# Selection matmuls beside the scores, lent PSUM banks, one routed group held back, zero matmuls at the start: sigmoid attention with mixture of depths

## The chip, the core and the metric

The kernel runs on one core of a Trainium2 chip. The time is device microseconds of one execution. Three runs of the kernel before gave 525.93, 521.94 and 525.99 us; the median is 525.93 us.

## The reference, cut to what matters

```python
# q, k, v: (8, 12, 448, 64) float32          B, H, S, Dh
scores = scale * (q @ k.transpose(0, 1, 3, 2)) - log(S)
attn   = 1 / (1 + exp(-scores))              # sigmoid, no softmax
x      = (attn @ v) transposed to (8, 448, 768)

# mixture of depths: per batch, 128 of the 448 tokens are routed
s   = x . w_gate                             # (8, 448)
top = the 128 tokens with the largest s
h   = relu(x[top] @ w1)                      # w1 768 x 1024
out = x;  out[top] = x[top] + sigmoid(s[top]) * (h @ w2)   # w2 1024 x 768
```

Everything is float32. The attention has 96 heads; the routed part has eight batches of 128 rows.

## The kernel before, in words

**Steps and units.** The work is written out by hand: every engine's instructions are issued in program order. Four heads of one batch make a group (24 groups, three to a batch), and two groups make a *step* (12 steps, numbered 0 to 11; what follows step 11 is called step 12). A step has seven *units*, numbered 0 to 6. `unit(s, n)` writes scores of 128 keys for four heads into two PSUM tiles of two banks each (16 matmuls; the trace counts each as two) and reads each tile with one sigmoid on ScalarE (L210). Units 0 to 2 belong to the step's first group, 4 to 6 to its second, unit 3 to both.

**Between the units.** `gap(s, n)` puts other TensorE work behind unit n: in gaps 0 to 2 the rest of the attention times v of the step before (`values`, L237), in gaps 3 to 5 routed work, in gap 6 the first part of `values` of this step. `values` fills two PSUM tiles o0 and o1; after its last part VectorE reads them (`take`, L252) and they are free again. PSUM holds four such tiles in all: two that rotate for the scores (`psc`), and o0 and o1, which `values` and the routed work share. `banks("o")` hands out o0 and o1 in turn. In step 0 units 1, 3 and 5 use o0 and o1 for their scores.

**Routing of a batch b.** When its third group is done, `store` writes x to a scratch in HBM and to the output (8 DMAs on SyncE's queue) and `gate` makes the scores. In gaps 4 to 6 of the same step (batch 0: 5 and 6) follow `spread` (one matmul, L289), `rank` for four blocks of tokens (two VectorE instructions each, L306 and L309) and `place` (builds the 0/1 matrix `sel`, L318). In the next step comes `select`: four small matmuls with `sel` (L326), then on VectorE the row numbers `row` and `idx` (L329, L331), on ScalarE the gate (L333), and on GpSimd's queue the gather of the 128 rows (`xe`, L335). Before the change `select` takes a `psc` tile of its own, behind unit 0. `turn_rows` then transposes the rows (L345) and copies them (L347), and six routed groups follow, kept in the list `ready`: three of `ffn1` (L357, relu L359) and three of `ffn2` (L366, added to `xe` on VectorE, L368). The last one scatters the rows to the output (L372). `go` issues the next group of the list.

**VectorE's other work.** `turn(i)` transposes q and k of group i (L181 to L184); unit 0 of a step needs `turn(2s)`, unit 3 needs `turn(2s + 1)`. It is called behind unit 5 (for the next step) and behind unit 1. Tiles `row`, `idx`, `gate` and `xe` have two buffers each, so those of batch b wait until the scatter of batch b - 2 is done.

Of the kernel before, what the change touches and what calls it, by code (L numbers as in the profile page):

```python
# [17 lines left out]
def kernel(  # L18
# [11 lines left out]
    nc = tc.nc  # L30
# [40 lines left out]
    ps_sc = ctx.enter_context(tc.tile_pool(name="ps_sc", bufs=2, space=PSUM))  # L71
    ps_o = [ctx.enter_context(tc.tile_pool(name=f"ps_o{n}", bufs=1, space=PSUM))
            for n in range(2)]
    turns = [0]

    def banks(which):
        if which == "psc":
            return ps_sc.tile([P, 2, 512], F32, name="psc")
        if which == "o":
            turns[0] ^= 1  # L80
            which = turns[0]
        return ps_o[which].tile([P, 2, 512], F32, name=f"o{which}")
# [60 lines left out]
    def constants():  # L143
        nc.gpsimd.memset(ones, 1.0)
        make_identity(nc, iden)
        for a in range(4):
            p = slice(a * TT, (a + 1) * TT)
            nc.gpsimd.dma_start(
                out=wg_b[p],
                in_=bass.AP(tensor=moe_w_gate.tensor, offset=moe_w_gate.offset + a * TT,  # L150
                            ap=[[0, TT], [P, HP], [1, TT]]))
        nc.gpsimd.iota(iota_r, pattern=[[1, CAP]], base=0, channel_multiplier=0,
                       allow_small_or_imprecise_dtypes=True)
        for t in (above, level, sel):
            nc.gpsimd.memset(t, 0.0)
        for t in tok_gate:
            nc.gpsimd.memset(t, 0.0)
            for a in range(4):
                nc.gpsimd.iota(t[a * TT:(a + 1) * TT, :, 0], pattern=[[4, NC]], base=a,
                               channel_multiplier=TB, allow_small_or_imprecise_dtypes=True)  # L160
        number = moe.tile([P, TB, TT], F32, name="rep")
        nc.gpsimd.iota(number, pattern=[[1, TB], [TB, TT]], base=0, channel_multiplier=0,
                       allow_small_or_imprecise_dtypes=True)
        for c in range(NC):
            nc.gpsimd.tensor_scalar(
                out=earlier[:, c, :], in0=number.rearrange("p r t -> p (r t)"),
                scalar1=tok_gate[0][:, c, 0:1], scalar2=None, op0=ALU.is_lt)
# [4 lines left out]
    def turn(i):  # L172
# [8 lines left out]
            nc.vector.transpose(kT[i][:, e, :HK],  # L181
                                sk[:, e, :HK].rearrange("p (m c) d -> p c m d", c=NF))
        nc.vector.transpose(kT[i][:, :, HK:], sk[:, :, HK:])
        nc.vector.transpose(qT[i], sq)  # L184

    def unit(s, n):


        if s == 0 and n in (1, 3, 5):
            psc = [banks(0), banks(1)]  # L190
        else:
            psc = [banks("psc"), banks("psc")]
# [5 lines left out]
        for e in range(2):  # L198
            for y, (x, r) in enumerate(parts):
                for h in range(4):  # L200
# [3 lines left out]
                        kT[2 * s + x][d, e, r:r + 2, :].rearrange("d r t -> d (r t)"),  # L204
                        qT[2 * s + x][d, e].rearrange("d r t -> d (r t)"),
                        start=(e == 0), stop=(e == 1))
        for pr in range(2):
            a = attnp.tile([P, 2, S], F32, name=f"attn{pr}", bufs=NU + 3)
            attn[s, pr, n] = a
            nc.scalar.activation(a, psc[pr][:, :, :S], AF.Sigmoid, bias=bias_s, scale=QK_SCALE)  # L210

    x_tiles, gate_parts, st = {}, {}, {}
    def values(s, n):
# [104 lines left out]
            nc.vector.tensor_scalar(out=sel[:n, c], in0=iota_r[:n], scalar1=pl[:n, c:c + 1],  # L318
                                    scalar2=None, op0=ALU.is_equal)

    def select(b, s0, n, where="o"):

        tg = tok_gate[b % 2]
        pk = banks(where)[:, 0]
        for c in range(NC):
            nc.tensor.matmul(pk[:n, 0:2], sel[:, c, s0:s0 + n], tg[:, c, :],  # L326
                             start=(c == 0), stop=(c == NC - 1))
        row = moe.tile([P, 1], I32, name="row", bufs=2)
        nc.vector.tensor_copy(row[:n], pk[:n, 0:1])  # L329
        idx = moe.tile([P, 1], I32, name="idx", bufs=2)  # L330
# [9 lines left out]
    def turn_rows(b, n, where="o"):  # L340
        xeT = moe.tile([P, 2, KD // 2, P], F32, name="xeT")
        ps = banks(where).rearrange("p a (k n) -> p a k n", n=P)
        for t in range(KD):
            a, i = divmod(t, KD // 2)
            nc.tensor.transpose(ps[:, a, i, :n], st[b]["xe"][:n, t * P:(t + 1) * P],  # L345
                                iden[:n, :n])
        nc.scalar.activation(xeT[:, :, :, :n], ps[:, :, :KD // 2, :n], AF.Copy)  # L347
        st[b]["xeT"] = xeT.rearrange("p a k n -> p (a k) n")

    def ffn1(b, n, f0, f1, where):  # L350
# [37 lines left out]
            fn, args = ready.pop(0)  # L388
            fn(*args, where)

    early, late = {}, {}

    def put(where, s, n, fn, *args):
        where.setdefault((s, n), []).append((fn, args))
# [5 lines left out]
    def routed(b):  # L400

        s = (NG * b + NG - 1) // 2 + 1
        at = 5 if b == 0 else 4
        put(late, s, at, spread, b)
        for c in range(NC - 1):
            put(late, s, at, rank, b, c)
        put(late, s, 6, rank, b, NC - 1)
        put(late, s, 6, place, b)
        if s == NS:
            return  # L410
        for s0, n in SLOTS:
            put(early, s + 1, 0, select, b, s0, n, "psc")
            put(late, s + 1, 3, turn_rows, b, n)
            put(late, s + 1, 3, routed_groups, b, n)

# [5 lines left out]
            gate(b)  # L421

    def gap(s, n):
        due(early, s, n)
        if n < 3 and s > 0:
            values(s - 1, n + 1)
            if n == 2:
# [1 line left out]
        if 3 <= n < NU - 1:  # L429
            if not ready:  # L430
                due(late, s, n)
            go()
            if n == NU - 2 and s < NS - 2:
                go()
        if n == NU - 1 and s < NS:
            values(s, 0)
# [4 lines left out]
    def stream():  # L441
        for b in range(B):
            routed(b)
        load(0)
        load(1)
        nc.vector.memset(bias_s, NEG_LOG_S)
        turn(0)
        load(2)
        load_v(0)
        constants()  # L450
        for s in range(NS):
            for n in range(NU):
# [12 lines left out]
                if n == NU - 2:  # L465
                    turn(2 * s + 2)
                    load(2 * s + 4)

        for n in range(5):
            gap(NS, n)  # L470
        for n in range(3):
            go()
        due(late, NS, NU - 1)
        for s0, n in SLOTS:
            select(B - 1, s0, n)
        while ready:
            go()
        for s0, n in SLOTS:
            turn_rows(B - 1, n)
            routed_groups(B - 1, n)  # L480
        while ready:
            go()
        assert not early and not late

    with tc.manual_schedule():
        stream()
# [29 lines left out]
```

## Time and profile before

| | |
|---|---|
| runs | 525.93, 521.94, 525.99 us |
| profiled execution | 521.8 us, span 520.0 us, mean granted TensorE clock 0.978 |
| TensorE busy | 476.0 us (92%) |
| VectorE, ScalarE, GpSimd busy | 210.9, 189.8, 27.3 us |
| moved by DMA | 68.67 MB, mean 132 GB/s |

The span runs from the first to the last instruction; the profiled execution took 1.8 us more than its span. A timeline row says when a run of like instructions started, how long it took, and in brackets how long its engine stood idle before it and what ended that. Matmuls are pipelined, so TensorE can be busy and yet slow: the granted clock and the duration of equal work tell that apart.

### The profile page before, as it was taken

The numbers are of one execution on the slowest core, as the hardware profiler recorded it, in microseconds if no ns is written. First come the engines' busy times: TensorE is split into PE (matmuls) and PEld (weight loads), VectorE is DVE, ScalarE is ACT, GpSimd is POOL, SyncE is SP. The second block draws the span as 40 slices with busy tenths as digits, with TensorE's granted clock in tenths as the row PEclk, the third lists the DMA queues.
The fourth block names the chain that finished last, engine by engine and source line by source line (L and its number), as shares of the span: only waits on it lengthen the run. The fifth ranks groups of instructions, "written<-read, shape, count | busy, mean of one in ns | idle before, by whom it ended". The sixth has DMA issues, their size and how long they took to land. (4 is left out here: it accounts for less than half of the span.)

```text
span 520.0 us, 14605 instructions
## 1 busy us (share of the span) xinstructions
PE 476.0 (92%) x6656; PEld 304.6 (59%) x6656; DVE 210.9 (41%) x458; ACT 189.8 (36%) x253; POOL 27.3 (5%) x46
## 2 busy tenths in 40 slices
PE   4997986989999999989999999989999999897895
PEld 1462723467468456457457557457557566486794
DVE  3305166155452156354533155543535156272101
ACT  2845443332442442434343343354343444010010
POOL 8000000000000000100000000100000000000100
PEclk9999997889999999999999999999999999999799
DMA  8909298897752077878744048858834037385100
GB/s 265 221 24 337 79 271 151 166 311 122 179 142 102 3 166 122 183 176 127 170 84 168 3 104 161 191 124 164 159 83 138 3 55 126 68 129 114 36 26 30
DMA packets 203421, 68.67 MB, mean 132 GB/s; under 512 B 182048, under 2 KB 194400, under 8 KB 203360
## 3 DMA queue, kind: packets, MB, share of 16 engines
q1 hardware_dynamic: 201952, 61.36, 53.4%
q0 software_dynamic: 1408, 6.39, 3.9%
q8 instruction: 52, 0.85, 0.7%
q14 instruction: 9, 0.07, 0.0%
HBM read 42.57 MB, written 25.17 MB: 130 GB/s over the span
## 5 line engine op out<-in xcount | busy, mean ns | idle before, releaser
L210 ACT ACTIVATE attn<-psc,bias_s 128x896 f32<-128x896 f32 x162 | 154.4, 1004 | 148.9 <-PE psc L202 148.9
L202 PE MATMUL psc<-qT,kT 32*64 32x448 f32 x2592 | 155.0, 551 | 16.0 <-DVE qT L184 10.2
L237 PE MATMUL o<-attn,raw_v 32*64 32x448 f32 x2304 | 132.8, 542 | 0.8 <-ACT o L240 0.8
L202 PEld LDWEIGHTS psc<-qT,kT 32*64 32x64 f32 x2592 | 60.0, 133 | 83.8 <-issue 50.1
L357 PEld LDWEIGHTS o<-xeT,w_sb 128*128 128x128 f32 x768 | 88.7, 195 | 19.6 <-issue 7.8
L357 PE MATMUL o<-xeT,w_sb 128*128 128x128 f32 x768 | 92.1, 280 | 8.9 <-ACT xeT L347 6.7
L366 PE MATMUL o<-w_sb,hT 128*128 128x256 f32 x384 | 89.9, 391 | 6.0 <-ACT gate L333 4.5
L366 PEld LDWEIGHTS o<-w_sb,hT 128*128 128x128 f32 x384 | 73.2, 195 | 24.8 <-issue 6.6
L237 PEld LDWEIGHTS o<-attn,raw_v 32*64 32x64 f32 x2304 | 57.0, 133 | 51.0 <-issue 43.3
L252 DVE STREAM_TRANSPOSE x_b<-o 128x448 f32<-128x448 f32 x48 | 26.9, 617 | 124.4 <-PE o L237 98.8
L181 DVE STREAM_TRANSPOSE kT<-raw_k 128x384 f32<-128x384 f32 x48 | 24.7, 554 | 43.4 <-PE psc L202 26.7
L368 DVE SCALAR_TENSOR_TENSOR xe<-o,gate,xe 128x256 f32<-128x256 f32 x24 | 11.6, 483 | 60.5 <-PE o L366 60.5
L359 ACT ACTIVATE hT<-o 128x384 f32<-128x384 f32 (+1 forms) x24 | 10.9, 456 | 65.0 <-PE o L357 65.0
L265 DVE TENSOR_REDUCE gate_p<-scr 128x14 f32<-128x896 f32 x24 | 26.1, 1087 | 0.8
L237 PE MATMUL o<-attn,raw_h 32*64 32x448 f32 x384 | 26.1, 537 | 0.0
L184 DVE STREAM_TRANSPOSE qT<-raw_q 128x896 f32<-128x896 f32 x24 | 25.7, 1071 | 0.5 <-DMA raw_q<-in_q_dram 0.5
L259 DVE TENSOR_TENSOR scr<-x_b,wg_b 128x896 f32<-128x896 f32 x24 | 25.6, 1066 | 0.1
L240 ACT ACTIVATE o<-bias_s 1x1 f32<-1x1 f32 x36 | 5.9, 165 | 49.5 <-PE o L237 35.1
L309 DVE SCALAR_TENSOR_TENSOR scr<-rep,tok_gate,earlier 128x448 f32<-128x448 f32 (+1 forms) x32 | 21.8, 683 | 1.1
L306 DVE TENSOR_SCALAR_CACHE_REDUCE scr<-rep,tok_gate 128x448 f32<-128x448 f32 (+1 forms) x32 | 21.4, 669 | 0.9
L335 POOL DMA_INDIRECT xe<-x_d,row x8 | 8.0, 994 | 246.7 <-DVE idx L331 204.5
L372 POOL DMA_INDIRECT out_dram<-xe,idx x8 | 7.9, 990 | 240.9 <-DVE xe L368 95.2
(48 smaller groups left out, 132.2 us busy)
## 6 DMA issues: line engine op xcount, KB each, us to landing
raw_k<-in_k_dram SPq DMA_DIRECT2D x24, 448.0 KB, 4.6
raw_q<-in_q_dram SPq DMA_DIRECT2D x24, 448.0 KB, 5.0
x_d<-x_b SPq DMA_DIRECT2D x32, 336.0 KB, 6.9
out_dram<-x_b SPq DMA_DIRECT2D x32, 336.0 KB, 6.5
raw_v<-in_v_dram SPq DMA_DIRECT2D x48, 192.0 KB, 3.6
w_sb<-in_moe_w_dram SPq DMA_DIRECT2D x6, 512.0 KB, 6.1
w_sb<-in_moe_w_dram SPq DMA_DIRECT2D x8, 384.0 KB, 4.5
raw_h<-in_v_dram SPq DMA_DIRECT2D x48, 32.0 KB, 4.4
```

The source lines that it names most:

```text
L181: nc.vector.transpose(kT[i][:, e, :HK], sk[:, e, :HK].rearrange("p (m c) d -> p c m d", c=NF))
L184: nc.vector.transpose(qT[i], sq)
L202: nc.tensor.matmul(psc[h // 2][y * Dh:(y + 1) * Dh, h % 2, :S], kT[2 * s + x][d, e, r:r + 2, :].rearrange("d r t -> d (r t)"), qT[2 * s + ...
L210: nc.scalar.activation(a, psc[pr][:, :, :S], AF.Sigmoid, bias=bias_s, scale=QK_SCALE)
L237: nc.tensor.matmul(o[x][j * Dh:(j + 1) * Dh, pr, :S], w, a[rows, j, :], start=(n == 0 and c == 0), stop=(n == 3 and c == NF - 1))
L252: nc.vector.transpose(x_tiles[b][:, :, 2 * g + pr, :], outs[s][x][:, pr, :S].rearrange("p (r t) -> p r t", t=TT))
L259: nc.vector.tensor_tensor(out=tmp, in0=x_tiles[b][:, :, 2 * g:2 * g + 2, :].rearrange("p r h d -> p r (h d)"), in1=wg_b[:, 2 * g:2 * g + 2 ...
L265: nc.vector.tensor_reduce(out=gate_parts[b][:, :, g], in_=tmp, axis=AX.X, op=ALU.add)
L306: nc.vector.tensor_scalar(out=junk[:n], in0=rep[:n], scalar1=own, scalar2=0.0, op0=ALU.is_gt, op1=ALU.add, accum_out=above[:n, c:c + 1])
L309: nc.vector.scalar_tensor_tensor(out=junk[:n], in0=rep[:n], scalar=own, in1=earlier[:n, c, :], op0=ALU.is_equal, op1=ALU.mult, accum_out=l ...
L357: nc.tensor.matmul(ps[:, f - f0, :n], w1_sb[:, t, f * P:(f + 1) * P], xeT[:, t, :n], start=(t == 0), stop=(t == KD - 1))
L366: nc.tensor.matmul(ps[:n, :ND], st[b]["hT"][:, t, :n], w2_sb[:, t, cols], start=(t == 0), stop=(t == KF - 1))
```

## The change

1. At the start `sel` is set to zero on VectorE instead of GpSimd, and TensorE multiplies it with itself three times (128x128 by 128x512) into o1. The first q is transposed in two halves.
2. Unit 4 of steps 1 and 2 writes its scores into o0 and o1 instead of `psc`.
3. `select` of batches 0 to 5 no longer takes a tile. It is issued right behind the scores of unit 0 (batch 0: unit 1), into two spare columns of that unit's first score bank. `row`, `idx`, gate and gather come behind the first of the unit's two sigmoids.
4. The first three `rank` blocks of batch 0 are issued behind `turn(6)` instead of ahead of it.
5. In gap 5 of steps up to 9 the second routed group is issued only if another one is left behind it.
6. From step 12 on the routed work takes `psc` tiles and o0/o1 alternately (`"any"`), and the copy of the last batch's transposed rows is shared by ScalarE and VectorE.

```diff
     def banks(which):
+        if which == "any":
+            turns[1] ^= 1
+            which = "psc" if turns[1] else "o"
...
-        for t in (above, level, sel):
+        for t in (above, level):
             nc.gpsimd.memset(t, 0.0)
...
-        nc.vector.transpose(qT[i], sq)
+        if i == 0:
+            for e in range(2):
+                nc.vector.transpose(qT[i][:, e], sq[:, e])
+        else:
+            nc.vector.transpose(qT[i], sq)
 
     def unit(s, n):
-        if s == 0 and n in (1, 3, 5):
+        if (s == 0 and n in (1, 3, 5)) or (s in (1, 2) and n == NF + 1):
             psc = [banks(0), banks(1)]
...
+        more = beside.pop((s, n), [])
+        for fn, args in more:
+            fn(*args, psc[0][:, 0, S:])
         for pr in range(2):
...
             nc.scalar.activation(a, psc[pr][:, :, :S], AF.Sigmoid, bias=bias_s, scale=QK_SCALE)
+            if pr == 0:
+                for fn, args in more:
+                    fetch(*args, psc[0][:, 0, S:])
...
-    def select(b, s0, n, where="o"):
+    def select(b, s0, n, pk):
         tg = tok_gate[b % 2]
-        pk = banks(where)[:, 0]
         for c in range(NC):
             nc.tensor.matmul(pk[:n, 0:2], sel[:, c, s0:s0 + n], tg[:, c, :],
                              start=(c == 0), stop=(c == NC - 1))
+
+    def fetch(b, s0, n, pk):
         row = moe.tile([P, 1], I32, name="row", bufs=2)
...
-        nc.scalar.activation(xeT[:, :, :, :n], ps[:, :, :KD // 2, :n], AF.Copy)
+        if where == "any":
+            nc.scalar.activation(xeT[:, 0, :, :n], ps[:, 0, :KD // 2, :n], AF.Copy)
+            nc.vector.tensor_copy(xeT[:, 1, :, :n], ps[:, 1, :KD // 2, :n])
+        else:
+            nc.scalar.activation(xeT[:, :, :, :n], ps[:, :, :KD // 2, :n], AF.Copy)
...
-        at = 5 if b == 0 else 4
-        put(late, s, at, spread, b)
+        put(late, s, 5 if b == 0 else 4, spread, b)
         for c in range(NC - 1):
-            put(late, s, at, rank, b, c)
+            put(late, s, 6 if b == 0 else 4, rank, b, c)
...
-            put(early, s + 1, 0, select, b, s0, n, "psc")
+            if s + 1 < NS:
+                put(beside, s + 1, 1 if b == 0 else 0, select, b, s0, n)
...
-            go()
-            if n == NU - 2 and s < NS - 2:
+            go("any" if s == NS else "o")
+            if n == NU - 2 and s < NS - 2 and len(ready) > 1:
                 go()
...
         load(1)
+        nc.vector.memset(sel, 0.0)
         nc.vector.memset(bias_s, NEG_LOG_S)
...
         load_v(0)
+        warm = banks(1)
+        for _ in range(3):
+            nc.tensor.matmul(warm[:, 0], sel[:, 0, :], sel.rearrange("p c n -> p (c n)"),
+                             start=True, stop=True)
...
+        def choose(b):
+            for s0, n in SLOTS:
+                pk = banks("psc")[:, 0]
+                select(b, s0, n, pk)
+                fetch(b, s0, n, pk)
+
+        choose(B - 2)
         for n in range(5):
             gap(NS, n)
         for n in range(3):
-            go()
+            go("any")
         due(late, NS, NU - 1)
+        choose(B - 1)
+        while ready:
+            go("any")
...
-            turn_rows(B - 1, n)
+            turn_rows(B - 1, n, "any")
```

Line numbers of the changed kernel are higher by up to 29; the names stay.

VectorE behind unit 5 of step 2, before the change (from the transposed token scores of batch 0 to `sel`):

```order
L298 COPY tok_gate_96<-scr 32x3 x2
L306 TENSOR_SCALAR scr,above<-rep,tok_gate_96 128x448
L309 SCALAR_TENSOR_TENSOR scr,level<-rep,tok_gate_96,earlier 128x448
...
L181 STREAM_TRANSPOSE kT<-raw_k 128x384 x2
L183 STREAM_TRANSPOSE kT<-raw_k 128x2x64
L184 STREAM_TRANSPOSE qT<-raw_q 128x896
L306 TENSOR_SCALAR scr,above<-rep,tok_gate_96 64x448
L309 SCALAR_TENSOR_TENSOR scr,level<-rep,tok_gate_96,earlier 64x448
L315 TENSOR_TENSOR place<-above,level 128x4
L318 TENSOR_SCALAR sel<-iota_r,place 128x128 x3
```

The same stretch with the change:

```order
L311 COPY tok_gate_96<-scr 32x3 x2
L184 STREAM_TRANSPOSE kT<-raw_k 128x384 x2
L186 STREAM_TRANSPOSE kT<-raw_k 128x2x64
L191 STREAM_TRANSPOSE qT<-raw_q 128x896
L319 TENSOR_SCALAR scr,above<-rep,tok_gate_96 128x448
L322 SCALAR_TENSOR_TENSOR scr,level<-rep,tok_gate_96,earlier 128x448
...
L319 TENSOR_SCALAR scr,above<-rep,tok_gate_96 64x448
L322 SCALAR_TENSOR_TENSOR scr,level<-rep,tok_gate_96,earlier 64x448
L328 TENSOR_TENSOR place<-above,level 128x4
L331 TENSOR_SCALAR sel<-iota_r,place 128x128 x3
```

The transposes of q and k for step 3 now stand ahead of the three full pairs of `rank` instead of behind them.

TensorE in gaps 3 and 4 of step 6, before the change (o0 and o1 are the two tiles that `values` has just left; the rows of unit 4 between are left out):

```order
L345 MATMUL o0_2520<-iden_90,xe_2352 128x128 x6
L357 MATMUL o1_2529<-xeT_2519,w1_sb_87 128x128 x18
...
L357 MATMUL o0_2587<-xeT_2519,w1_sb_87 128x128 x18
L289 MATMUL o1_2607<-rep_2563,ones_92 128x448
...
L357 MATMUL o0_2651<-xeT_2519,w1_sb_87 128x128 x12
```

The same with the change:

```order
L384 MATMUL o1_2510<-w2_sb_88,hT_1801 128x256 x8
L359 MATMUL o0_2522<-iden_90,xe_2331 128x128 x6
...
L375 MATMUL o1_2569<-xeT_2521,w1_sb_87 128x128 x18
L302 MATMUL o0_2589<-rep_2544,ones_92 128x448
...
L375 MATMUL o1_2633<-xeT_2521,w1_sb_87 128x128 x18
L375 MATMUL o0_2653<-xeT_2521,w1_sb_87 128x128 x12
```

The held group (the last `ffn2` of batch 1) now runs ahead of the transposes, in o1, and the first `ffn1` of batch 2 is no longer right behind the transposes that it needs.

ScalarE at the end, before the change (`hT` is the relu of an `ffn1` group of batch 6, `gate` that of batch 7):

```order
L292 ACTIVATE rep<-o_4894 128x448
L359 ACTIVATE hT<-o_4917 128x384
L359 ACTIVATE hT<-o_4937 128x384
L359 ACTIVATE hT<-o_4957 128x256
L333 ACTIVATE gate<-o_4981 128x1
L347 ACTIVATE xeT<-o_5026 128x768
```

The same with the change:

```order
L305 ACTIVATE rep<-o_4882 128x448
L377 ACTIVATE hT<-o_4916 128x384
L377 ACTIVATE hT<-psc 128x384
L347 ACTIVATE gate<-psc 128x1
L377 ACTIVATE hT<-o_4979 128x256
L362 ACTIVATE xeT<-o_5025 128x384
```

The third relu of batch 6 now stands behind the gate of batch 7.

## Rows read from the trace of the kernel before

**Rows 1.** The page: part 1, and three rows of part 5 (busy, mean | idle).

```profile
PE 476.0 (92%) x6656; PEld 304.6 (59%) x6656; DVE 210.9 (41%) x458; ACT 189.8 (36%) x253; POOL 27.3 (5%) x46
...
L237 PE MATMUL o<-attn,raw_v 32*64 32x448 f32 x2304 | 132.8, 542 | 0.8 <-ACT o L240 0.8
L357 PE MATMUL o<-xeT,w_sb 128*128 128x128 f32 x768 | 92.1, 280 | 8.9 <-ACT xeT L347 6.7
L366 PE MATMUL o<-w_sb,hT 128*128 128x256 f32 x384 | 89.9, 391 | 6.0 <-ACT gate L333 4.5
```

**Rows 2.** Waits of TensorE: who, for what, us in total, times, longest us.

```profile
PE psc L202 <- DVE qT L184: 10.2, 2, 6.5
PE o L357 <- ACT xeT L347: 6.7, 4, 1.9
PE psc L202 <- ACT attn L210: 5.8, 6, 1.1
...
PE psc L326 <- ACT attn L210: 4.5, 4, 1.1
PE psc L326 <- issue: 2.3, 2, 1.2
PE o L357 <- DVE x_b L252: 2.2, 2, 1.1
```

**Rows 3.** Timeline of the start: start us, us, engine, what [idle before].

```profile
5.41 1.07 DVE L184 STREAM_TRANSPOSE qT<-raw_q 128x896 f32<-128x896 f32 x1
...
6.54 3.29 PE L202 MATMUL psc<-qT,kT 32*64 32x448 f32 x32 [6.54 <-DVE qT L184]
...
9.91 1.91 ACT L210 ACTIVATE attn<-psc,bias_s 128x896 f32<-128x896 f32 x2 [7.68 <-PE psc L202]
...
12.56 1.69 PE L202 MATMUL psc<-qT,kT 32*64 32x448 f32 x32
...
12.84 1.91 ACT L210 ACTIVATE attn<-o,bias_s 128x896 f32<-128x896 f32 x2 [1.02 <-PE o L202]
```

**Rows 4.** Windows: stretch, length, engines' busy us, PEclk, DMA share, GB/s.

```profile
6.54:9.58 3.04, 3.04 (x32) 1.17 (x40) 1.80 (x4) 0.00 (x0) 2.88 (x3) 1.00 1.02 338
...
84.21:94.45 10.24, 8.35 (x80) 4.13 (x88) 5.21 (x16) 2.08 (x3) 1.11 (x1) 0.50 0.80 128
```

**Rows 5.** Timeline of step 1: VectorE's reads of o0 and o1, and unit 4.

```profile
37.80 2.24 DVE L252 STREAM_TRANSPOSE x_b<-o 128x448 f32<-128x448 f32 x4 [13.34 <-PE o L237]
...
40.26 2.65 PE L202 MATMUL psc<-qT,kT 32*64 32x448 f32 x32 [1.14 <-ACT attn L210]
```

**Rows 6.** Timeline, end of step 2 to unit 4 of step 3.

```profile
78.33 0.68 DVE L306 TENSOR_SCALAR_CACHE_REDUCE scr<-rep,tok_gate 128x448 f32<-128x448 f32 x1
...
82.57 1.03 DVE L181 STREAM_TRANSPOSE kT<-raw_k 128x384 f32<-128x384 f32 x2
...
84.94 3.29 PE L202 MATMUL psc<-qT,kT 32*64 32x448 f32 x32 [3.66 <-DVE qT L184]
...
86.31 0.86 DVE L318 TENSOR_SCALAR sel<-iota_r,place 128x128 f32<-128x128 f32 x4
...
113.66 1.76 PE L202 MATMUL psc<-qT,kT 32*64 32x448 f32 x32
```

**Rows 7.** Timeline of SyncE's queue: the store of batch 0 to scratch.

```profile
73.42 13.18 SPq L273 DMA_DIRECT2D x_d<-x_b  x4
```

**Rows 8.** DMA issues, 65 to 135 us: xcount, KB each, us to landing.

```profile
x_d<-x_b SPq DMA_DIRECT2D x8, 336.0 KB, 7.2
...
xe<-x_d,row POOLq DMA_INDIRECT x1, 5.7
```

**Rows 9.** Timeline of the end.

```profile
478.35 0.99 POOL L372 DMA_INDIRECT out_dram<-xe,idx  x1 [33.95 <-DMA out_dram<-x_b]
481.42 0.16 DVE L331 TENSOR_SCALAR idx<-o 128x1 int32<-128x1 f32 x1 [7.43 <-DMA out_dram<-xe,idx]
...
481.89 9.67 PE L366 MATMUL o<-w_sb,hT 128*128 128x256 f32 x32 [4.54 <-ACT gate L333]
```

More of the change, by code (lines that the diff above doesn't have):

```diff
@@ L73 @@
             for n in range(2)]
-    turns = [0]
+    turns = [0, 0]
     def banks(which):
+        if which == "any":
+            turns[1] ^= 1
+            which = "psc" if turns[1] else "o"
         if which == "psc":
@@ L389, in go @@
             fn(*args, where)
-    early, late = {}, {}
+    late = {}
+    beside = {}
     def put(where, s, n, fn, *args):
@@ L423, in gap @@
     def gap(s, n):
-        due(early, s, n)
         if n < 3 and s > 0:
@@ L471, in stream @@
         for n in range(3):
-            go()
+            go("any")
         due(late, NS, NU - 1)
+        choose(B - 1)
+        while ready:
+            go("any")
         for s0, n in SLOTS:
[L475 to L478, printed above, removed]
-            turn_rows(B - 1, n)
+            turn_rows(B - 1, n, "any")
             routed_groups(B - 1, n)
         while ready:
-            go()
-        assert not early and not late
+            go("any")
+        assert not late and not beside
     with tc.manual_schedule():
```

## The prediction, made before the changed kernel was run

> **What bounds the kernel now.** I read part 1 of the page first: TensorE is busy for 92% of the span, no other engine for more than 41% [rows 1]. So the end is set by TensorE's own order of work, and the change can gain only where TensorE stands idle or runs slowly. Its list of waits [rows 2] gives the idle places: 10.2 us for transposed q, 6.7 us for the copied rows in front of `ffn1`, 5.8 us for score tiles that ScalarE has not yet read, 6.8 us in front of `select`, 2.2 us for o tiles that VectorE has not yet read. The timeline of the start [rows 3] shows something that no wait shows: the first unit's scores take 3.29 us and the third's 1.69 us for the same 32 matmuls, so TensorE runs at half speed for its first 6.0 us (6.54 to 12.56). The windows [rows 4] show a later stretch of 10.24 us at a granted clock of 0.50, the 1.2 GHz level. Its work began after 3.66 us of idleness for transposed q [rows 6]. The times below are the old trace's own, each step counted from its old start, so that the shifts add.
>
> **Start: -2.5 us.** `sel` is zeroed while the first loads are on their way, so this costs nothing on VectorE. The three zero matmuls can start when that is done, which I put at 1.4 us. If half speed again lasts 6.0 us from the first work on [rows 3], it ends at 7.4 us instead of 12.5. The halved q transpose lets the scores start 0.5 us earlier (half of 1.07 us, [rows 3]). Unit 0 then ends near 8.4 instead of 9.9, and the 1.02 us that ScalarE waits for unit 1 [rows 3] goes too. Step 0 is paced by ScalarE (two sigmoids, 1.91 us a unit), so both pass on: 1.5 + 1.0 = 2.5. Bounds: full speed at once gives 3.3; zero matmuls that change nothing in the clock and outlast the transposes cost 0.5. The removed memset on GpSimd is worth nothing, since TensorE needs `sel` only in step 3. The window of the first scores prints a granted clock of 1.00 while they take double time [rows 4]; by that print the zero matmuls would buy nothing, and I go by the durations. The Trainium skill, page "TensorE: Matmul & The Clock Gate", section "What's actually happening", calls the low clock the default from which activity releases the engine; by that rule the term is -2.5, by the printed clock -0.5 (the q halves alone).
>
> **Step 1, unit 4 in lent tiles: -3.6 us.** Units 4 to 6 have no other work between them, so each waits for the sigmoids of the one before: a unit every 3.8 us (2.65 busy and 1.14 idle, [rows 5]). With o0 and o1, unit 4 waits for VectorE's reads instead (37.80 + 2.24 = 40.04, [rows 5]), hardly earlier than its old 40.26. But unit 5 then finds the `psc` tiles free and follows at once (41.4 to 43.0). The sigmoids run back to back, 1.91 us a unit, and unit 6 ends at 46.8 instead of 40.26 + 2 x 3.76 + 2.65 = 50.4 (3.76 from 2.65 and the 1.11 that the other idle places have).
>
> **Steps 2 and 3: -9.5 us.** The same in step 2 gives -3.5, and `spread`, the copies and the first `rank` come 3.3 us earlier, at 75.0 instead of 78.3 [rows 6]. Now `turn(6)` follows at once (2.2 us, up to 84.8 in the old order, [rows 6]) and is done at 77.2. TensorE ends unit 6 at 74.5 and the part of `values` behind it at 77.5 (132.8 us for 48 parts are 2.8 each, [rows 1], and this part also works off the shared unit 3), so unit 0 of step 3 starts at 77.5 instead of 84.94 [rows 6], without idleness and so without the slow stretch. `rank` and `place` end where they would have: the whole chain of `rank`, `turn` and `place` takes 87.17 - 78.33 = 8.84 us [rows 6], so `sel` is ready at 83.8. `select`, now behind unit 1, is reached at 83.6: no wait worth a number, where behind unit 0 it would have waited 5 us. Unit 3 then ends at 92.9. What is late next is the gather: the store to scratch is paced by DMA, its last issue leaves at about 83.3 (three quarters of 13.18 us after 73.42, [rows 7]) and lands 7.2 us later [rows 8]; the gather takes 5.7 us from there [rows 8], to 96.2. TensorE waits 3.3 us for it (before, the gather was hidden). Transposes, copy and `ffn1` bring unit 4 to 102.2, and I add 2.0 for a slow stretch behind that wait, half of an `ffn1` group: 104.2 instead of 113.66 [rows 6]. Bounds: -11.5 without a slow stretch, -3 if VectorE's chain ends 3 us late again.
>
> **`select` beside the scores, batches 1 to 5: -5.7 us.** Of the 6.8 us in front of `select` [rows 2], 1.1 belong to batch 0, counted above; the other five waits of 1.1 us go, since no tile is waited for. The price: the unit's first sigmoid starts behind `select` (1.0 us), then `row`, `idx` and the gate stand ahead of the second. From the end of `select`, ScalarE needs two sigmoids (1.91, [rows 3]) and VectorE and ScalarE three small instructions of 0.16 us (the one of [rows 9]), 2.4 us in all; TensorE spends 2.8 us on `values` before unit 1 wants the tiles, so I take it as hidden. Bounds: 0, if ScalarE's delay comes back as the same wait, and -6.8.
>
> **The held group in steps 5 to 11: +0.6 us.** It moves one group (3.7 us, [rows 1]: 89.9 / 24) from step 5 to the end, and puts a group ahead of the transposes in steps 6 and 9: two waits of 1.9 us for the copy go (6.7 us over 4, [rows 2]). But o0 and o1 are handed out in turn, and by the new order the first group of gap 3 draws o1, which VectorE frees last, in steps 5, 6, 7, 9, 10 and 11: six waits of 1.1 us [rows 2] where there were two. -3.8 - 2.2 + 6.6 = +0.6.
>
> **The end: 0.** The first group takes a `psc` tile and no longer waits for VectorE. But the next wait hangs on a DMA: batch 5's scatter waits 33.95 us for the stores of batch 7, `idx` of batch 7 waits for that scatter, and the gate waits for `idx` [rows 9]. The hold ends at about 481.8, counted from the last `values`, in both kernels. Before, two routed groups were left then in front of the last transposes. Now the third relu of batch 6 stands behind the gate on ScalarE, so three are left: +3.7, against -3.7 for the group that came out of step 5; the relu ahead of them and the shortened copy about cancel. TensorE idles about 6 us there instead of 4.54, with the same slow stretch behind it. The other `"any"` tiles hide behind groups of 3.7 us.
>
> **Sum.** -2.5 - 3.6 - 9.5 - 5.7 + 0.6 + 0 = -20.7; 521.8 - 20.7 = 501.1. The profiled run is 4.1 us below the median of the three (525.93), and no row says why; I add 0.9: **502 us**, own range 497 to 507, chance 0.55.
>
> **Rivals.**
> - *VectorE stays the bound in steps 2 and 3* (0.18). `turn(6)` is done 0.3 us before it is wanted, `sel` 0.2 us after. If the chain runs 3 us late, TensorE idles as before and the slow stretch returns: 8 us of the 9.5 are lost, 510 us. For: two margins below half a us. Against: all durations are from the same rows.
> - *Zero matmuls do nothing* (0.10): +3.0 instead of -2.5 plus 0.5, 505 us. For: the printed clock [rows 4].
> - *The held group covers the end* (0.08). If the hold ends before TensorE needs the relu, 6 us of idleness and the slow stretch (9.67 us for two groups, against 7.4, [rows 9, 1]) go: 502 - 8.3 = 494 us. Against: a wait of 33.95 us on a store that nothing speeds up.
> - *Select in front of everything* (0.03). `select` now stands on TensorE ahead of `values` and, in its bank, ahead of the unit's first sigmoid. If `sel` were late by L in each of six steps, both engines would wait L; from L = 3.7 on (the 3.66 us of [rows 6]) a slow stretch worth about 4.5 us follows each time. 6 x (3.7 + 4.5) = 49, so 550 us, slower; at L = 3 it is 18 us and still faster. In the old order only batch 0's `sel` was late, so it is unlikely.
> - *Several gains fail together* (0.06): within 1% of 526.
>
> **How the numbers follow.** The range takes in the forecast, the rivals at 494, 505 and 510, and the bounds of the start: 493 to 511. Below 520.7 counts as faster, above 531.2 as slower (1%, what a measurement can tell): faster 0.91, same 0.06, slower 0.03.
>
> **What would show it.** Step 0: first sigmoid near 8.4 us, scores of 1.7 us from the second unit on. Steps 1 and 2: unit 5 right behind unit 4, no 1.1 us waits for `attn`. Step 3: no wait for transposed q, a wait of some 3 us for `xe`. Later steps: no wait before `select`; six waits of 1.1 us for `x_b`. End: `gate` still ended by the scatter, and 6 us of idleness on TensorE in front of `ffn2`. I am wrong if the waits for q stay, if `select` waits for `sel`, or if the idleness at the end goes.

## The result and the profile after

Four runs of the changed kernel gave a median of 502.26 us (501.37 to 503.83), the kernel before 525.96 us beside them. The ratio is 0.956 with a 95% interval of 0.950 to 0.962: faster, and within 0.3 us of the forecast of 502. The terms did not come out as well as their sum. The profiled execution took 502.38 us (before: 521.8). Of the runs of the experiments below one, of u_rank, took 974.98 us; it counts as slow and is left out of that kernel's ratio (the median of its other three runs is 502.46 us).

Parts 1 and 2 of the page after, busy us (share of the span) and the granted clock in 40 slices; the first row answers to [rows 1].

```profile
PE 473.4 (95%) x6662; PEld 307.7 (61%) x6662; DVE 211.8 (42%) x461; ACT 189.3 (38%) x253; POOL 28.0 (6%) x45
...
PEclk9998999799999999999999999999999999999899
```

The waits of TensorE after (us in total, times, longest), as in [rows 2]:

```profile
PE o L359 <- DMA xe<-x_d,row: 4.7, 1, 4.7
PE psc L384 <- ACT hT L377: 4.5, 1, 4.5
PE o L384 <- DVE x_b L265: 4.3, 4, 1.1
PE o L375 <- DVE x_b L265: 2.2, 2, 1.1
...
PE psc L209 <- ACT attn L220: 1.4, 1, 1.4
```

The waits for transposed q and those in front of `select` are gone. New are the wait for the gathered rows `xe` and four more waits for `x_b`, six in all, as the prediction counted them.

The timelines after, of the start [rows 3], of unit 6 of step 1 [rows 5], of the end of step 2 to unit 4 of step 3 [rows 6] and of the end [rows 9]. A row gives start us, us, engine, what, and in brackets the idle time before it.

```profile
1.45 4.72 PE L471 MATMUL o<-sel 128*128 128x512 f32 x6 [1.45 <-DVE bias_s L465]
6.10 1.76 PE L209 MATMUL psc<-qT,kT 32*64 32x448 f32 x32
...
7.93 1.90 ACT L220 ACTIVATE attn<-psc,bias_s 128x896 f32<-128x896 f32 x2 [5.15 <-PE psc L209]
...
41.64 3.24 PE L209 MATMUL psc<-qT,kT 32*64 32x448 f32 x26 [1.40 <-ACT attn L220]
...
72.01 1.07 DVE L191 STREAM_TRANSPOSE qT<-raw_q 128x896 f32<-128x896 f32 x1
...
80.20 1.05 PE L338 MATMUL psc<-tok_gate,sel 128*128 128x2 f32 x8
...
93.88 1.41 PE L359 MATMUL o<-iden,xe 128*128 128x128 f32 x6 [4.66 <-DMA xe<-x_d,row]
96.19 6.48 PE L375 MATMUL o<-xeT,w_sb 128*128 128x128 f32 x36 [0.90 <-ACT xeT L365]
102.61 1.76 PE L209 MATMUL psc<-qT,kT 32*64 32x448 f32 x32
...
431.81 2.24 DVE L265 STREAM_TRANSPOSE x_b<-o 128x448 f32<-128x448 f32 x4 [8.93 <-PE o L250]
...
455.58 2.76 PE L384 MATMUL psc<-w_sb,hT 128*128 128x256 f32 x12
...
459.04 0.99 POOL L390 DMA_INDIRECT out_dram<-xe,idx  x1 [34.99 <-DMA out_dram<-x_b]
...
462.35 0.17 ACT L347 ACTIVATE gate<-psc 128x1 f32<-128x1 f32 x1 [9.65 <-DVE idx L345]
462.42 0.38 ACT L377 ACTIVATE hT<-o 128x256 f32<-128x256 f32 x1
...
462.85 2.07 PE L384 MATMUL psc<-w_sb,hT 128*128 128x256 f32 x4 [4.51 <-ACT hT L377]
...
472.29 0.82 PE L359 MATMUL o<-iden,xe 128*128 128x128 f32 x6
```

Windows after, as [rows 4]: the three stretches at the 1.2 GHz level, each behind one of the waits above. By the two levels, a stretch in which TensorE is busy throughout costs half its length, which is an estimate.

```profile
42.81:46.22 3.41, 3.41 (x48) 1.40 (x39) 0.58 (x1) 0.58 (x1) 0.00 (x0) 0.50 1.03 418
94.01:100.84 6.83, 5.93 (x28) 5.53 (x28) 1.23 (x3) 0.81 (x1) 0.00 (x0) 0.50 0.88 204
462.65:466.06 3.41, 3.21 (x8) 2.55 (x9) 0.48 (x1) 0.15 (x1) 0.97 (x1) 0.50 0.40 115
```

Where the 19.4 us came from is read at fixed points of the work, before against after: the first `take` of step 1 (37.80 and 34.68), that of step 2 (65.65 and 61.20), unit 4 of step 3 (113.66 and 102.61), the last `take` (452.12 and 431.81), TensorE's last matmul (514.5 and 495.1).

| stretch | forecast | measured |
|---|---|---|
| start, step 0 | -2.5 | -3.1 |
| step 1 | -3.6 | -1.3 |
| steps 2 and 3, to unit 4 | -9.5 | -6.6 |
| from there to the last `take` (`select` -5.7, held group and bank order +0.6, the group itself -3.7) | -8.8 | -9.3 |
| end | +3.7 | +0.9 |

The forecast's 0 for the end was +3.7 - 3.7; the second stands in the fourth row here, since that group left the steps ahead of the last `take`.

The table adds up to the 19.4 us between the two profiled executions, while the medians are 23.7 us apart, because the profiled execution before is 4.2 us below its median. No trace shows these 4 us. Over the runs of the kernel before, however, the time goes with the mean granted clock (519.59 us at 0.981, 526.0 at 0.972, 528.49 at 0.966), so much of it is likely to be half clock that comes in some executions and not in others.

### The profile page after: what moved, and what is told of

It is laid out like the page before. It is cut to its first block, busy times and chain, and to the rows that moved or that the text cites. A ratio compares the mean times of both kernels' runs of the same rounds, so it can differ in the third digit from the quotient of the medians.

```text
span 500.6 us, 14613 instructions
## 1 busy us (share of the span) xinstructions
PE 473.4 (95%) x6662; PEld 307.7 (61%) x6662; DVE 211.8 (42%) x461; ACT 189.3 (38%) x253; POOL 28.0 (6%) x45
## 5 line engine op out<-in xcount | busy, mean ns | idle before, releaser
L220 ACT ACTIVATE attn<-psc,bias_s 128x896 f32<-128x896 f32 x158 | 151.1, 1003 | 129.8 <-PE psc L209 116.4
L209 PE MATMUL psc<-qT,kT 32*64 32x448 f32 x2528 | 149.4, 545 | 1.4 <-ACT attn L220 1.4
L250 PEld LDWEIGHTS o<-attn,raw_v 32*64 32x64 f32 x2304 | 58.8, 133 | 50.3 <-issue 41.9
L375 PEld LDWEIGHTS o<-xeT,w_sb 128*128 128x128 f32 x672 | 78.8, 197 | 12.9 <-issue 6.4
L375 PE MATMUL o<-xeT,w_sb 128*128 128x128 f32 x672 | 81.6, 282 | 3.1 <-DVE x_b L265 2.2
L384 PE MATMUL o<-w_sb,hT 128*128 128x256 f32 x304 | 70.4, 386 | 4.3 <-DVE x_b L265 4.3
L384 PEld LDWEIGHTS o<-w_sb,hT 128*128 128x128 f32 x304 | 57.1, 192 | 21.0 <-PE psc L209 7.3
L386 DVE SCALAR_TENSOR_TENSOR xe<-o,gate,xe 128x256 f32<-128x256 f32 x19 | 9.2, 483 | 55.4 <-PE o L384 55.4
L384 PE MATMUL psc<-w_sb,hT 128*128 128x256 f32 x80 | 19.4, 395 | 4.5 <-ACT hT L377 4.5
L307 DVE STREAM_TRANSPOSE scr<-o 128x448 f32<-128x448 f32 x8 | 5.2, 650 | 37.2 <-ACT rep L305 37.2
```

The source lines that it names most:

```text
L209: nc.tensor.matmul(psc[h // 2][y * Dh:(y + 1) * Dh, h % 2, :S], kT[2 * s + x][d, e, r:r + 2, :].rearrange("d r t -> d (r t)"), qT[2 * s + ...
L250: nc.tensor.matmul(o[x][j * Dh:(j + 1) * Dh, pr, :S], w, a[rows, j, :], start=(n == 0 and c == 0), stop=(n == 3 and c == NF - 1))
L375: nc.tensor.matmul(ps[:, f - f0, :n], w1_sb[:, t, f * P:(f + 1) * P], xeT[:, t, :n], start=(t == 0), stop=(t == KD - 1))
L384: nc.tensor.matmul(ps[:n, :ND], st[b]["hT"][:, t, :n], w2_sb[:, t, cols], start=(t == 0), stop=(t == KF - 1))
```

## The experiments

Twelve kernels, all made from the changed one. The ratio is to the kernel before, run beside them.

| run | median us | ratio, 95% interval |
|---|---|---|
| the change | 502.26 | 0.956 (0.950 to 0.962) |
| u_nowarm | 503.91 | 0.962 (0.954 to 0.969) |
| u_owntile | 510.92 | 0.974 (0.967 to 0.981) |
| u_rank | 502.83 | 0.958 (0.950 to 0.966) |
| u_nolend | 500.96 | 0.957 (0.950 to 0.964) |
| u_ranklend | 506.76 | 0.968 (0.961 to 0.975) |
| u_noreserve | 505.59 | 0.960 (0.957 to 0.963) |
| u_oend | 499.61 | 0.952 (0.948 to 0.957) |
| x_bank | 496.52 | 0.944 (0.939 to 0.949) |
| x_idx3 | 496.16 | 0.942 (0.939 to 0.945) |
| x_rows0 | 498.79 | 0.947 (0.943 to 0.950) |
| x_two_nolend | 488.28 | 0.933 (0.926 to 0.940) |
| x_three | 483.63 | 0.924 (0.917 to 0.932) |

The kernel before took 523.8 to 527.2 us (medians) beside them, so differences of up to some 3 us lie inside these intervals; for them the traces decide.

### The start: u_nowarm

```diff
-        warm = banks(1)
-        for _ in range(3):
-            nc.tensor.matmul(warm[:, 0], sel[:, 0, :], ...)
```

> The changed kernel without its three zero matmuls; `sel` is still zeroed on VectorE and the first q still transposed in halves. Theory (the zero matmuls bring TensorE to the 2.4 GHz level before the first scores, and step 0 is paced by ScalarE, so what is gained there stays): the first three or so units take double time again, the first sigmoid comes near 9.4 us instead of 7.93, unit 1 is waited for again, and the takes of step 1 come 2.5 to 3 us later; time near 505 us. Rival (the early clock is the same with or without them, and the 3.1 us at the takes of step 1 came from the q halves and the q loads): within 0.5 us at the takes of step 1, 502 to 503 us.

Measured: 503.91 us, and every `take` from step 4 on 2.05 us later than with the zero matmuls. The timeline of its start:

```profile
6.10 3.29 PE L209 MATMUL psc<-qT,kT 32*64 32x448 f32 x32 [6.10 <-DVE qT L189]
9.14 2.50 PE L209 MATMUL o<-qT,kT 32*64 32x448 f32 x32
...
9.47 1.90 ACT L220 ACTIVATE attn<-psc,bias_s 128x896 f32<-128x896 f32 x2 [6.70 <-PE psc L209]
```

The scores start at 6.10 us in both kernels; without the work ahead of them the same 32 matmuls take 3.29 instead of 1.76 us. The clock records of the traces agree: the first one, at full clock, begins at 10.8 us here, at 5.3 us in the change and at 12.5 us in the kernel before, and the 1.00 that a window prints ahead of it only means that there is no record yet.

The theory holds, but its size is less sure than this pair of traces makes it look. In all twelve traces with the zero matmuls the sigmoids of unit 6 of step 0 start at 19.1 to 20.2 us, here at 21.08. But the first `take` of step 1 comes at 34.68 to 36.81 us in those twelve, the change's own being the earliest, and at 36.70 here. At that point the gain is between 0 and 2 us, 1.3 in the mean.

### `select` in the scores' bank: u_owntile

```diff
-        for fn, args in more:
-            fn(*args, psc[0][:, 0, S:])
         for pr in range(2):
...
+        for fn, args in more:
+            pk = banks("psc")[:, 0]
+            fn(*args, pk)
+            fetch(*args, pk)
```

> The changed kernel with `select` again in a `psc` tile of its own, drawn behind both sigmoids of the same unit. Theory (the gain of 5.7 us is the wait for a score tile, not the place in the order): a wait of about 1.1 us for ScalarE's `attn` stands in front of `select` in each of the six steps, 6 x 1.1 = 6.6 us, less 1.1 in step 3 if the gather's wait takes it up; 507.5 to 509 us. Rival (any tile will do once `select` stands behind a unit, and the waits merely move to the next unit): within 1 us of 502.

Measured: 510.92 us, 8.7 more and above what I expected. The six waits are there, 6.9 us together, and half clock follows some of them; timeline and window behind one:

```profile
195.32 1.06 PE L337 MATMUL psc<-tok_gate,sel 128*128 128x2 f32 x8 [1.13 <-ACT attn L218]
196.31 3.29 PE L249 MATMUL o<-attn,raw_v 32*64 32x448 f32 x32
```

```profile
196.30:199.60 3.30, 3.30 (x41) 1.39 (x48) 2.35 (x6) 0.17 (x1) 0.98 (x1) 0.50 0.82 127
```

Behind three of the six waits TensorE runs at half clock for 3.4 us, 1.7 us lost each time; in the kernel before this did not happen behind the waits of batches 1 to 5. That makes 12.0 us. Against it, this trace lacks the change's slow stretch in step 1 (1.7), and its wait for `xe` with the stretch behind it is 3.6 us cheaper; the stretch at the end costs 1.7 more. Together 8.5 of the 8.9 us between the two traces. `select` stands behind the same scores on TensorE in both, so the tile, not the place in the order, is what counts.

### Steps 1 to 3: u_rank, u_nolend, u_ranklend

```diff
-            put(late, s, 6 if b == 0 else 4, rank, b, c)
+            put(late, s, 5 if b == 0 else 4, rank, b, c)
```

> The changed kernel with the first three `rank`s of batch 0 back ahead of `turn(6)`. Theory (two limits stand one behind the other in step 3, transposed q first and the gather second): q of step 3 is ready about 4.2 us later (three `rank`s of some 1.4 us), so unit 0 of step 3 starts near 77.4 us instead of 73.23 behind a wait of some 3.5 to 4 us; but the gather lands where it did, near 93.8, so its wait of 4.66 us shrinks by as much, and unit 4 of step 3 starts within 0 to 3.5 us of its 102.61 (3.5 if a stretch of half clock follows the q wait as in the kernel before). Time 502 to 506 us. Rival (the order of the ranks alone carries the gain of steps 2 and 3): all 4.2 us and the slow stretch reach unit 4, 106.8 or later, and the time is 507 us or more.

```diff
-        if (s == 0 and n in (1, 3, 5)) or (s in (1, 2) and n == NF + 1):
+        if s == 0 and n in (1, 3, 5):
```

> The changed kernel with unit 4 of steps 1 and 2 in `psc` tiles again. Theory: the waits of 1.1 us for `attn` return in front of units 5 and 6 of both steps, and unit 6 of step 1 starts behind an idle place as before, without the half-clock stretch of 42.8 to 46.2 us; so step 1 costs 1.3 us more (what it gained, measured at the takes of step 2), step 2 about 3.5 us more at unit 0 of step 3. Part of that is taken up by the gather's wait only if the store to scratch does not come later with it; the store hangs on the takes of step 2, so it does: 505 to 507 us. Rival (the lent tiles gain nothing, because VectorE's reads of them bind instead): 502 to 503 us.

u_ranklend is both edits.

> The changed kernel with two parts undone together, each of which changed the time by under 1.5 us alone: the first three `rank`s of batch 0 ahead of `turn(6)`, and unit 4 of steps 1 and 2 in `psc` tiles. Theory (each of the two by itself gives the transposed q of step 3 its slack, so either suffices, and the term of 9.5 us for steps 2 and 3 is lost only without both): q is ready about 4.3 us later than in the run without the lent tiles (77.8 + 4.3 = 82.2), TensorE waits about 4 us for it with a stretch of half clock behind, `select` comes near 88.5 and the gather lands near 96.5, when unit 3 ends too: unit 4 of step 3 starts at 106 to 110 instead of 102.6; 505 to 510 us. Rival (the gather alone sets step 3, the order on VectorE does not matter): 501 to 503 us.

Measured: 502.83, 500.96 and 506.76 us. Alone neither part is worth anything that can be measured; both together are worth 4.5 us. The waits of u_rank, u_nolend and u_ranklend in this order, those of steps 1 to 3 (in u_nolend neither q nor `xe` is waited for):

```profile
PE psc L209 <- DVE qT L191: 3.7, 1, 3.7
```

```profile
PE psc L209 <- ACT attn L220: 5.8, 6, 1.1
...
PE o L375 <- ACT xeT L365: 1.9, 1, 1.9
```

```profile
PE psc L209 <- ACT attn L220: 5.8, 6, 1.1
...
PE psc L209 <- DVE qT L191: 3.7, 1, 3.7
```

Unit 4 of step 3 in the same three runs:

```profile
103.22 1.76 PE L209 MATMUL psc<-qT,kT 32*64 32x448 f32 x32
```

```profile
100.43 1.76 PE L209 MATMUL psc<-qT,kT 32*64 32x448 f32 x32
```

```profile
108.16 1.76 PE L209 MATMUL psc<-qT,kT 32*64 32x448 f32 x32
```

In u_rank the wait for q is back, and the wait of 4.66 us for `xe` is gone: the gather is issued at 88.2 us as in the change, and TensorE waits either here or there. In u_nolend TensorE reaches unit 0 of step 3 later, so q is in time although the slow units are back, and the gather is no longer waited for: unit 4 of step 3 comes 2.2 us earlier than with lent tiles (100.43 and 102.61), as this trace has no stretch of half clock in steps 1 to 3. My expectation for u_nolend was wrong by 4 to 6 us: I charged steps 1 and 2 with their own loss and did not let the gather's wait pay for it. In u_ranklend q is late, `select` is late behind it, and unit 4 of step 3 starts at 108.16 instead of 102.61.

### What the gather hides: x_rows0

```diff
-            put(late, s + 1, 3, turn_rows, b, n)
-            put(late, s + 1, 3, routed_groups, b, n)
+            put(late, s + 1, 4 if b == 0 else 3, turn_rows, b, n)
+            put(late, s + 1, 4 if b == 0 else 3, routed_groups, b, n)
```

> The changed kernel with batch 0's transposes and routed groups one gap later, in gap 4 of step 3, behind unit 4. Theory (the gather, bound by the store to scratch, swallows what the lent tiles and the earlier q gained; work that does not need it takes the wait up): unit 4 follows unit 3 after 1.1 us for ScalarE, the transposes still wait about 1.2 us for the gather that lands at 93.8, 2.3 us of idleness instead of 4.66, and the stretch of half clock behind it, 6.8 us long, goes or gets shorter: 496.5 to 500 us. Rival (the group that is left over is paid for later, since every gap already holds one): 502 to 504 us.

Measured: 498.79 us. Timeline of its step 3, unit 4 and the transposes:

```profile
90.89 2.65 PE L209 MATMUL psc<-qT,kT 32*64 32x448 f32 x32 [1.85 <-ACT attn L220]
94.03 0.85 PE L359 MATMUL o<-iden,xe 128*128 128x128 f32 x6 [0.49 <-DMA xe<-x_d,row]
...
96.24 4.29 PE L375 MATMUL o<-xeT,w_sb 128*128 128x128 f32 x36
```

Work that does not need the gather takes half of the idleness up (2.64 us are left of 5.56), and in this trace no stretch of half clock follows: 36 matmuls in 4.29 us where the change needs 6.48. The rival had a point too: this trace is 8.0 us ahead at the first `take` of step 4 but 4.6 us from step 6 on, since the group left over is worked off in between. Of the lead, 1.7 us are the slow stretch of step 1, which did not come here; a start 1.5 us later than the change's takes as much away again.

### The held group and the bank order: u_noreserve, x_bank

```diff
-            if n == NU - 2 and s < NS - 2 and len(ready) > 1:
+            if n == NU - 2 and s < NS - 2:
```

> The changed kernel without the rule that holds one routed group back (`len(ready) > 1` taken out). Theory: three things move. The transposes of steps 6 and 9 again stand right ahead of their `ffn1`, two waits of 1.9 us for the copy, +3.8; the first group of gap 3 again draws o0 in all but two steps, -4.4; and at the end all three relus of batch 6 stand ahead of the held gate on ScalarE, so the three `ffn2` groups (11 us) fill the hold up to 462, and TensorE next waits for the gather of batch 7, which lands 3.8 us after its issue behind the hold, at about 466.6 instead of transposes at 472.3, -5.5. Sum -6: 495 to 499 us. Rival (the reserve pays for itself, as my sum of +0.6 - 0 said): 501.5 to 503 us.

```diff
+        if n == 3 and s < NS:
+            turns[0] = 1
         if 3 <= n < NU - 1:
```

> The changed kernel with one line more: ahead of gap 3 of each step the turn is set so that the first routed group draws o0, which VectorE frees first. Theory: the six waits of 1.1 us for `x_b` in steps 5, 6, 7, 9, 10 and 11 go, and nothing else stands in their place, -6.6, less up to 1 where a group now waits for the copy out of the other bank: 495 to 497 us. Rival (VectorE's four reads bind whichever bank comes first, or each wait turns into one at the next unit): 501 to 503 us.

x_bank gave 496.52 us: the waits for `x_b` are gone and nothing took their place, 5.7 of the 6.6 us in the median. Its longest wait of TensorE and its third; none for `x_b` is left:

```profile
PE o L359 <- DMA xe<-x_d,row: 5.1, 1, 5.1
...
PE psc L209 <- ACT attn L220: 1.9, 2, 1.4
```

u_noreserve gave 505.59 us, 3.3 more where I expected 3 to 7 less; by the ratios the 3.3 lie inside the intervals, so the trace has to show where they are. The waits came out as I had counted them (two for `x_b`, two of 1.9 us for the copy). What I missed stands in the timeline of its end:

```profile
459.19 3.70 PE L384 MATMUL o<-w_sb,hT 128*128 128x256 f32 x16
...
465.43 0.99 POOL L390 DMA_INDIRECT out_dram<-xe,idx  x1 [34.20 <-DMA out_dram<-x_b]
469.21 0.97 POOL L349 DMA_INDIRECT xe<-x_d,row  x1 [2.79 <-DVE xe L386]
...
473.16 1.51 PE L359 MATMUL psc<-iden,xe 128*128 128x128 f32 x6 [3.36 <-DMA xe<-x_d,row]
```

`ffn2` does run through the hold. But the hold follows the last `take`s, since it ends when batch 7's rows are stored; these came 7.1 us later, and the scatter 6.4 us later than with the reserve. A group held back is thus not only work for the end, it also lets the stores start earlier. Of the 7.8 us lost between steps 5 and 11, 3.5 are that group (a second group in a gap adds that much) and 1.7 a stretch of half clock behind one of the copy waits, while the other waits together are 0.6 shorter. Another 2.8 stand in two steps, 5 and 8, that took 39.8 us each, 1.4 more than in the kernel before without its wait for `select` (39.5 less 1.1), at full clock and with no new wait in the records; 0.4 remain. That is open.

### The end: x_idx3, u_oend

```diff
-        row = moe.tile([P, 1], I32, name="row", bufs=2)
+        row = moe.tile([P, 1], I32, name="row", bufs=3)
... (idx and gate likewise)
```

> The changed kernel with three buffers instead of two for the small tiles `row`, `idx` and `gate` (`xe` keeps two). Theory (the hold at the end runs from batch 5's scatter over `idx` of batch 7 and its gate to the relu behind it): `idx` and the gate no longer wait, the third relu of batch 6 comes at about 456, and TensorE runs its three `ffn2` groups without the 4.5 us of idleness and the half clock behind it; but the gather of batch 7 still needs the `xe` of batch 5 and lands at about 466, so the transposes start at 466 to 467.5 instead of 472.3: 496.5 to 498.5 us. Rival (the wait is not the hold of `idx` but the scatter's time on GpSimd's queue, which comes back at the transposes): 501 us or more.

Measured: 496.16 us; the profiled execution, 499.33, is the slowest of its five. Timeline of its end, of batch 7's gate, batch 6's third relu, batch 7's gather and its transposes:

```profile
455.89 0.17 ACT L347 ACTIVATE gate<-psc 128x1 f32<-128x1 f32 x1 [0.62 <-DVE idx L345]
458.36 0.38 ACT L377 ACTIVATE hT<-o 128x256 f32<-128x256 f32 x1 [2.29 <-PE o L375]
...
465.22 0.97 POOL L349 DMA_INDIRECT xe<-x_d,row  x1 [2.78 <-issue]
...
469.19 0.84 PE L359 MATMUL o<-iden,xe 128*128 128x128 f32 x6 [0.51 <-DMA xe<-x_d,row]
```

The gate no longer waits, and of the hold 0.51 us of idleness is left, for the gather that still needs batch 5's `xe`. From the last `take` to the end the kernel gained 5.6 us.

```diff
-            turns[1] ^= 1
-            which = "psc" if turns[1] else "o"
+            which = "o"
```

> The changed kernel with o tiles alone for all routed work behind the last unit (the `psc` tiles are used there for `select` only; the copy of the rows stays shared between ScalarE and VectorE). Theory (the end hangs on the hold behind batch 5's scatter, which no tile moves): the first group waits 1.1 us for `x_b`, and TensorE's idleness of 4.5 us in front of the last relu shrinks by as much; behind the hold the groups of 3.7 us hide each other's reads: 501.5 to 503 us, no change. Rival (two tiles are too few once ScalarE, VectorE and the held gate all read them): at least one more wait of 1 to 4 us at the end, 503.5 to 506 us.

Measured: 499.61 us, below both expectations; by its interval it can't be told from the change. Two of its waits, at the first group behind the last `take` and at the hold:

```profile
435.03 3.69 PE L383 MATMUL o<-w_sb,hT 128*128 128x256 f32 x16 [2.59 <-DVE x_b L264]
...
463.24 8.04 PE L383 MATMUL o<-w_sb,hT 128*128 128x256 f32 x36 [1.72 <-ACT hT L376]
```

It waits 2.59 us for `x_b` there and 1.72 instead of 4.51 us at the hold, behind which the clock does not fall this time. The alternating banks at the end gained nothing that can be measured.

### Together: x_three, x_two_nolend

x_three has the edits of x_bank, x_idx3 and x_rows0, x_two_nolend the first two and u_nolend.

> The changed kernel with the three edits that each gained alone: o0 first in gap 3, three buffers for `row`, `idx` and `gate`, batch 0's routed rows in gap 4 of step 3. Theory (they act in three separate stretches: steps 5 to 11, the end, step 3): the gains add, 502.3 - 5.7 - 6.1 - 3.5 = 487.0, 485.5 to 489 us. Rival (the end hangs on batch 7's stores, and the earlier last takes do not bring those forward by as much): 490 us or more.

> The changed kernel with o0 first in gap 3, three buffers for `row`, `idx` and `gate`, and unit 4 of steps 1 and 2 in `psc` tiles; batch 0's rows stay in gap 3. Theory (the lent tiles are worth nothing while the gather sets step 3, and something only once the rows stand a gap later): 501.0 - 5.7 - 6.1 = 489.2, 488 to 491 us, so 2 us above the run with the rows in gap 4 and the lent tiles. Rival (the lent tiles gain 3.6 us in step 1 and 3.5 us in step 2 as I predicted): 494 us or more.

Measured: 483.63 and 488.28 us. The waits left in x_three:

```profile
PE psc L209 <- ACT attn L220: 3.0, 3, 1.4
PE o L359 <- DVE gate_p L278: 1.5, 1, 1.5
PE o L473 <- DVE bias_s L467: 1.5, 1, 1.5
PE o L359 <- DMA xe<-x_d,row: 1.0, 1, 1.0
```

x_three is 3.4 us below the sum of the three gains, and below the range that I gave. Its trace has no stretch of half clock before 479 us, where each of the three parts alone still had one or more; that this is all of the 3.4 us is not shown. The 4.7 us between these two are batch 0's later rows, worth 3.5 alone, and the lent tiles together; how much of them the tiles have is not shown, since no run has the later rows without them.

## Why the prediction was right, and where it was not

**Bound and direction.** TensorE's order set the time, and the gain came from its idle places. (Of the 10.2 us for transposed q that the prediction lists among them, 6.5 are the start itself.) The rival without a gain from the zero matmuls (505 us) fell, and u_nowarm shows it at 503.9 us. The one in which VectorE stays the bound (510 us) fell too, and its price was wrong as well: in u_rank q is late by the same 3.66 us with a stretch of half clock behind it, and the time is still 502.8 us. It takes the lent tiles undone besides, in u_ranklend, to get 506.8 us.

**Start, -2.5.** Measured -3.1, the earliest of twelve traces with the same start (1.0 to 3.1). Against u_nowarm 2.05 of it are the zero matmuls (0 to 2 over the twelve); the other 1.1 is what u_nowarm still has over the kernel before, and no run takes that apart. Full clock came at 5.3 us, not at the 7.4 of the sum. I went by durations and not by the printed clock, and that was right. By the Trainium skill, page "TensorE: Matmul & The Clock Gate", section "What's actually happening", the throttled clock is the default and activity releases it; the two timelines of the start agree (3.29 and 1.76 us for equal work), and the granted clock of 1.00 in the row of [rows 4] does not describe that stretch.

**Step 1, -3.6.** Measured -1.3. Unit 6 waited 1.40 us, and a stretch of 3.41 us at half clock came behind it: 1.7 us that no step of the prediction had. It is not tied to the code: of ten kernels with this same wait, four show the stretch, and in u_rank, without it, the step gains 3.0.

**Steps 2 and 3, -9.5: the mis-sized term.** q and `sel` came in time, as forecast (unit 0 of step 3 without a wait, `select` at 80.20). But the wait for `xe` was 4.66 us instead of 3.3, and the stretch behind it 6.83 us long, 3.4 us lost instead of the 2.0 that I had put there. The deeper error is in the adding: I priced the lent tiles at 3.6 + 3.5 us and the order on VectorE beside them. The runs show them as two ways to the same end. Either gives q its slack; then the gather, which the store to scratch and `row` bring to 93.8 us, is the next limit, and most of what steps 1 to 3 gain beyond it goes into waiting for it.

**`select`, -5.7.** The five waits went, no wait came back at the next unit, and ScalarE's delay is hidden, as reasoned. Undone, the six waits cost more than their length, because of the clock.

**Held group, +0.6.** The six waits of 1.1 us came where the order of the banks put them, the two waits for the copy went, and the stretch to the last `take` came out within 0.5 us. Yet the rule seems worth more than I gave it: without it the kernel is 3.3 us slower in the median and 3.2 us between the traces. I counted the group as 3.7 us moved from one place to another; it also moves the last stores, and the copy waits cost more than their length.

**End, +3.7 there and -3.7 earlier.** The hold stayed: the scatter, which `idx` of batch 7 waits for, was issued 26.2 us behind the last `take` before and 27.2 us behind it after, and the third relu stood behind the gate. I had three full groups left and 6 us of idleness. In the trace 12 of the 16 matmuls of the first `ffn2` ran under the hold (455.58, 2.76 us), since only the last blocks of `hT` need the third relu; 4.51 us of idleness and a shorter slow stretch remained, so this end costs 0.9 instead of 3.7. No run undoes the shared copy of the last rows; TensorE waits 0.64 us behind it, where it waited 0.96 before.

**The sum.** The 5.2 us too much in steps 1 to 3 were mostly made good by the end (2.8), the start (0.6) and the stretch to the last `take` (0.5). The sum was also counted from a profiled execution 4.1 us below its median, with 0.9 added for that without a row to show it. That the 502 is right to a fraction of a us is partly luck.

## What to carry to other kernels

When two edits remove the same wait, their gains do not add; look for the wait that ends next behind both, here a gather, and put work in front of it that does not need it. A tile that rotates can be drawn in an order that always waits for the slower reader: one line that resets the turn was worth 5.7 us. Small tiles deserve one more buffer than large ones, since a 512-byte index held the whole end for 4.5 us.

## What the runs showed of the hardware

- The half-clock stretches behind the start that ended within a trace lasted about 3.4, 6.8 or 10.2 us, behind waits of 1.1 to 5.2 us. The wait of 1.1 us in front of `select` was followed by one three times in six in u_owntile, and behind those of batches 1 to 5 in the kernel before not once. What decides it was not settled; a wait on TensorE should be priced at its length and at up to half of such a stretch more, an estimate of 1.7 to 5.1 us.
- The print of the granted clock is 1.00 from the start of a trace on, also where equal matmuls take twice their time. The clock records begin only where TensorE first comes to full clock, 4.3 to 12.5 us into these traces.
